# Spreading 1/den of a token chunk over the feature partitions: one DMA with a repeated source, in place of four DMAs with strided targets

## The chip, the cores and the metric

The kernel runs on one core of a Trainium2 chip. The metric is the time on the device in microseconds (us), the median of several executions. Next to each time stands the mean clock granted to TensorE, as a share of full speed. PE is TensorE's matmul side, PEld its weight loads, DVE is VectorE, ACT is ScalarE, SP is SyncE; SPq is the queue in which SP issues DMAs. L586 is line 586 of the kernel. In the profile's lines `ek` is the buffer that holds the result of the spread (`rdb(c)` is a slice of it), `ps<-W,HG` are the products with `W2`, and `ps<-Msb,PQ` the products with `PQ`.

## The reference, cut to what matters

A block of two parallel branches on a normalised input: a linear attention with 32 heads of width 20, and a dense layer of 1536 features with GELU. There are 2048 tokens of width 640, all in bf16.

```python
def _A_ref(x, wqkv, wo):                       # linear attention
    # ... q, k, v = split of x @ wqkv
    phi = lambda t: jnp.where(t > 0, t + 1, jnp.exp(t)) + 1e-6
    pq, pk = phi(q), phi(k)
    kv = jnp.einsum("bhsd,bhse->bhde", pk, v)
    z = jnp.einsum("bhsd->bhd", pk)
    num = jnp.einsum("bhqd,bhde->bhqe", pq, kv)
    den = jnp.einsum("bhqd,bhd->bhq", pq, z)[..., None] + 1e-6
    return (num / den) @ wo                    # heads joined again, cut here
# ...
xn = _layernorm(x)
return x + _A_ref(xn, A_wqkv, A_wo) + _B_ref(xn, B_w1, B_b1, B_w2, B_b2)
```

What matters here is `den`: one number for each token and head. Every feature of `pq` has to be multiplied by the 1/den of its head.

## The kernel before

The kernel holds `pq` transposed: features on the partitions, tokens along the row. The features are ordered so that partition p of each of the five tiles belongs to head p // 4. `den` comes out of a matmul with one head on one partition: rows 32c to 32c+31 of `rden` are the 32 heads of token chunk c (512 tokens). To scale `pq`, row h must reach the four partitions 4h to 4h+3. That is the spread. DMAs do it, on the SyncE queue:

```python
def den_step(b):
    # ... 20 matmuls give den for all four chunks in one bank, cut
    Pl.ins(v, lambda e: e.tensor_single_scalar(den_sb[:], bank(b), 1e-6, ALU.add), ...)   # arguments cut
    Pl.ins(v, lambda e: e.reciprocal(rden[:], den_sb[:]), reads=[r_den], writes=[r_rden])

def rden_scale(c):                       # VectorE: five pieces of 128 x 512
    cc = slice(c * CW, (c + 1) * CW)
    for j in range(DT):
        Pl.ins(v, lambda e, j=j: e.tensor_tensor(out=PQ[:, j, cc], in0=PQ[:, j, cc], in1=rdb(c), op=ALU.mult),
               reads=r_rdb[c] + [r_PQ[c][j]], writes=[r_PQ[c][j]])

def rden_dma(c):                         # SyncE: the spread
    for i in range(4):
        Pl.ins("sync", lambda e, i=i: e.dma_start(rdb(c)[i:P:4, :], rden[H * c:H * (c + 1), :]),
               reads=[r_rden], writes=[r_rdb[c][i]] + ([r_rdb[0][i]] if c == 3 else []), dma=True)
```

The order of work at the end of the kernel decides when the spread is wanted. A tile is 128 tokens; its output is twelve products with `W2` (dense branch), which need no `den`, and five with the scaled `PQ` (attention branch), each done as two matmuls. The `W2` products that PE can do while the spread is on its way are called its cover.

```python
m_step(bs[1:4])
den_step(bs[3])
for t in range(1, 4):
    out_w2(t, b=bs[t])            # W2 products of tiles 1, 2, 3: work that needs no den
ring[0] = bs[0]
rden_dma(0)
rden_scale(0)
rden_dma(1)
for t in range(4):
    out_fin(t, bs[t])             # PQ products of tiles 0 to 3, eviction, store
    if t == 2:
        rden_scale(1)
for t in range(4, NT - 1):
    b = out_w2(t)
    if t in (6, 10):
        rden_scale({6: 2, 10: 3}[t])
    out_fin(t, b)
    if t in (4, 7):
        rden_dma({4: 2, 7: 3}[t])
```

## Time and profile before

| | before |
|---|---|
| time, first 3 runs | 208.4 us (207.85 to 208.42) |
| span in the profile | 206.8 us, clock 1.00 |
| PE busy | 203.2 us, 98% |
| one DMA of the spread | 32 KB, 0.59 us to issue, lands after 1.9 us |

First, who is busy, and what ended last. From the page of the kernel before, parts 1 and 4 (busy time, share of the span and number of instructions; then the chain of work that ended last, by engine):

```profile
PE 203.2 (98%) x1588; PEld 140.3 (68%) x1588; DVE 112.3 (54%) x231; ACT 73.1 (35%) x141; POOL 21.1 (10%) x59
...
PE 96%; DMA 3%; ACTq 0%; DVE 0%; issue 0%
```

The chain is nearly all PE. Its 3% of DMA is the first load of weights; no `rden` DMA and no scaling is on it.

Then the stretch where the first spread happens. The timeline of the kernel before, of VectorE, SyncE and PE in turn (start in us, duration in us, engine, line, operation, number of instructions, and in brackets the idle time before and what ended it):

```profile
134.94 3.35 DVE L568 RECIPROCAL rden<-den_sb 128x512 bf16<-128x512 f32 x1
142.18 1.77 DVE L575 TENSOR_TENSOR PQ<-PQ,ek 128x512 bf16<-128x512 bf16 x5 [3.89 <-DMA ek<-rden]
...
138.32 5.01 SPq L586 DMA_DIRECT2D ek<-rden  x8
...
134.09 9.95 PE L615 MATMUL ps<-W,HG 128*128 128x320 bf16 x72
143.88 5.60 PE L615 MATMUL ps<-Msb,PQ 128*128 128x320 bf16 x40
```

The reciprocal ends at 138.29 us, SyncE issues eight DMAs in 5.01 us (chunks 0 and 1; about 0.63 us each), and VectorE waits 3.89 us for the first four. But PE has 72 matmuls of cover to do from 134.09 us, and goes over to the `PQ` products at 143.88 us with no bracket behind its line: it did not wait. The first scaled piece was ready at about 142.62 us (142.18 + 0.44).

The view of the DMAs of the kernel before has for each kind of issue its number, KB each and the median us from issue to landing:

```profile
DMA packets 24043, 18.32 MB, mean 89 GB/s; under 512 B 10584, under 2 KB 24024, under 8 KB 24024
...
ek<-rden SPq DMA_DIRECT2D x16, 32.0 KB, 1.9
```

The sixteen DMAs of the spread carry 512 KB of the 18.32 MB; each is small, and its 1.9 us can hardly be due to its size, as the 160 KB stores land after 1.8 us.

### The profile page before, as it was taken

What the parts mean: (1) busy time and instruction counts of PE and PEld (TensorE: products, weight loads), DVE (VectorE), ACT (ScalarE), POOL (GpSimd) and SP (SyncE); (2) the same over time, 40 slices, a digit from 0 to 9 for tenths busy, and PEclk for the clock granted to TensorE, in tenths of its full rate; (3) what the DMA queues carried; (4) which work ended last, traced back from release to release, by engine and by line L of the source; (5) the groups of instructions that cost most, each with busy time, mean ns of one, the idle gap of its engine ahead of it and who ended that gap; (6) DMA issues with size and microseconds to landing.
All of it is one profiled execution on the core that took longest, in us unless ns stands there. A gap on an engine that the chain in (4) does not pass through costs nothing.

```text
span 206.8 us, 3962 instructions
## 1 busy us (share of the span) xinstructions
PE 203.2 (98%) x1588; PEld 140.3 (68%) x1588; DVE 112.3 (54%) x231; ACT 73.1 (35%) x141; POOL 21.1 (10%) x59
## 2 busy tenths in 40 slices
PE   7999999999999999999999999999999999999996
PEld 2799987444457777777756556677777777777775
DVE  4589970000007888999288888574863522522332
ACT  2689887666676555111153554400000000000000
POOL 3235568000022000000000000000000000000000
DMA  5999668998000000000300001931111111001002
GB/s 173 338 355 116 105 128 108 376 318 310 3 0 0 0 0 3 0 3 0 63 0 5 0 0 25 373 117 50 64 66 57 56 47 56 32 32 36 32 32 63
DMA packets 24043, 18.32 MB, mean 89 GB/s; under 512 B 10584, under 2 KB 24024, under 8 KB 24024
## 3 DMA queue, kind: packets, MB, share of 16 engines
q1 hardware_dynamic: 23344, 17.57, 29.8%
q10 hardware_dynamic: 680, 0.49, 0.9%
q8 instruction: 12, 0.20, 0.4%
q14 instruction: 7, 0.06, 0.1%
HBM read 12.62 MB, written 2.62 MB: 74 GB/s over the span
## 4 chain that ended last, share of the span: by engine, by line
PE 96%; DMA 3%; ACTq 0%; DVE 0%; issue 0%
PE ps L615 34%; PE ps L352 25%; PE ps L473 11%; PE ps L512 11%; PE ps L524 10%; DMA W<-in_B_w_dram 3%; PE ps L651 2%; PE ps L551 1%; PE ps L533 1%; PE ps L562 1%; PE ps L382 0%; PE ps L336 0%; ACTq L233 0%; DVE out_sb L654 0%
## 5 line engine op out<-in xcount | busy, mean ns | idle before, releaser
L352 PE MATMUL ps<-xnT,W 128*128 128x128 bf16 (+2 forms) x435 | 52.0, 282 | 0.0
L615 PE MATMUL ps<-W,HG 128*128 128x320 bf16 x360 | 51.0, 299 | 0.0
L352 PEld LDWEIGHTS ps<-xnT,W 128*128 128x128 bf16 x435 | 35.5, 98 | 15.7
L615 PEld LDWEIGHTS ps<-W,HG 128*128 128x128 bf16 x360 | 35.1, 98 | 14.2 <-issue 0.4
L356 ACT ACTIVATE HG<-ps,b1c 128x128 bf16<-128x128 f32 (+2 forms) x87 | 40.0, 492 | 12.6 <-PE ps L352 10.4
L634 DVE TENSOR_TENSOR out_sb<-ps,xnT 128x640 bf16<-128x640 f32 x15 | 12.4, 825 | 33.8 <-PE ps L615 33.6
L460 ACT ACTIVATE ek<-ps 128x512 bf16<-128x512 f32 (+1 forms) x36 | 23.2, 644 | 20.3 <-PE ps L524 11.1
L461 DVE TENSOR_SCALAR ek<-ek 128x512 bf16<-128x512 bf16 (+1 forms) x36 | 10.9, 304 | 33.7 <-ACT ek L460 32.6
L615 PE MATMUL ps<-Msb,PQ 128*128 128x320 bf16 x150 | 22.3, 299 | 0.0
L524 PE MATMUL ps<-xnT,Wqkv 128*128 128x512 bf16 x100 | 21.9, 379 | 0.0
L473 PE MATMUL ps<-Wqkv,xnT 128*128 128x320 bf16 x160 | 21.9, 299 | 0.0
L512 PE MATMUL ps<-xPK,xn_tm 128*128 128x320 bf16 x160 | 21.9, 299 | 0.0
L473 PEld LDWEIGHTS ps<-Wqkv,xnT 128*128 128x128 bf16 x160 | 15.7, 98 | 6.2
L512 PEld LDWEIGHTS ps<-xPK,xn_tm 128*128 128x128 bf16 x160 | 15.7, 98 | 6.1
L615 PEld LDWEIGHTS ps<-Msb,PQ 128*128 128x128 bf16 x150 | 14.7, 98 | 5.7
L524 PEld LDWEIGHTS ps<-xnT,Wqkv 128*128 128x128 bf16 x100 | 11.7, 118 | 9.5
L308 DVE BATCH_NORM_STATS2 stats<-xPK 128x6 f32<-128x320 bf16 x32 | 13.6, 466 | 2.8 <-DMA xPK<-in_A_x_dram 2.7
L463 DVE SCALAR_TENSOR_TENSOR PQ<-ps,ek 128x512 bf16<-128x512 f32 x20 | 13.8, 692 | 2.1
L463 DVE SCALAR_TENSOR_TENSOR xPK<-ps,ek 128x640 bf16<-128x640 f32 x16 | 13.2, 825 | 1.7
L499 DVE TENSOR_TENSOR Msb<-Msb,xPK 128x640 f32<-128x640 f32 x14 | 11.6, 825 | 0.5
L318 POOL TENSOR_TENSOR rstd<-aggr,mhalf 128x1 f32<-128x1 f32 x16 | 9.1, 568 | 8.9 <-DVE aggr L316 8.9
L516 ACT ACTIVATE W<-ps 128x640 bf16<-128x640 f32 x5 | 3.5, 703 | 18.2 <-PE ps L512 18.2
(61 smaller groups left out, 93.4 us busy)
## 6 DMA issues: line engine op xcount, KB each, us to landing
xnT<-in_A_x_dram SPq DMA_DIRECT2D x4, 640.0 KB, 6.8
Wqkv<-in_A_wqkv_dram SPq DMA_DIRECT2D x3, 800.0 KB, 6.9
out_dram<-out_sb SPq DMA_DIRECT2D x15, 160.0 KB, 1.8
W<-in_B_w_dram SPq DMA_DIRECT2D x1, 1920.0 KB, 15.4
W<-in_B_w_dram SPq DMA_DIRECT2D x3, 480.0 KB, 7.2
xPK<-in_A_x_dram SPq DMA_DIRECT2D x2, 640.0 KB, 8.6
Wo<-in_A_wo_dram SPq DMA_DIRECT2D x1, 800.0 KB, 10.8
xPK<-in_A_x_dram SPq DMA_DIRECT2D x4, 160.0 KB, 4.3
```

The costliest lines, as they stand in the source:

```text
L308: Pl.ins(v, lambda e: e.bn_stats(stats[:, s, 6 * h:6 * h + 6], x_in[:, t, h * HW:(h + 1) * HW]), reads=[r_x[t]], writes=[r_stats[s][h]])
L352: Pl.ins("tensor", [(lambda e, k=k: e.matmul(bank(b, 0, w), W1[:, k, jb * P:(jb + 1) * P], xnT[:, k, tok], start=(k == 0), stop=(k == DT - ...
L356: Pl.ins("scalar", lambda e: e.activation(HG[:, jb, tok], bank(b, 0, w), ACT.Gelu_apprx_tanh, bias=b1c[:, jb:jb + 1]), reads=[B_[b], r_b1c ...
L460: Pl.ins("scalar", lambda e: e.activation(e2, src, ACT.Exp), reads=br, writes=[r_ek[s]])
L461: Pl.ins(v, lambda e: e.tensor_scalar(et, et, 1.0, 1e-6, ALU.min, ALU.add), reads=[r_ek[s]], writes=[r_ek[s]])
L463: Pl.ins(v, lambda e: e.scalar_tensor_tensor(out=d2, in0=src, scalar=0.0, in1=e2, op0=ALU.max, op1=ALU.add), reads=br + [r_ek[s]], writes= ...
L473: fns.append(lambda e, k=k, h=h, b=b, t=t: e.matmul(bank(b + h, 0, HW), xnT[:, k, t * P:(t + 1) * P], Wqkv[:, k, D + h * HW:D + (h + 1) * ...
L499: Pl.ins(v, lambda e, t=t: e.tensor_tensor(out=zsum, in0=zsum, in1=PK[:, t, :], op=ALU.add), reads=[r_PK[t], r_zsum], writes=[r_zsum])
L512: Pl.ins("tensor", [(lambda e, t=t, h=h, b=b, f=f: e.matmul(bank(b + h, 0, HW), xn_tm[:, t, f * P:(f + 1) * P], PK[:, t, h * HW:(h + 1) * ...
L524: Pl.ins("tensor", [(lambda e, k=k, j=j, b=b: e.matmul(bank(b), Wqkv[:, k, j:D:DT], xnT[:, k, cc], start=(k == 0), stop=(k == DT - 1))) fo ...
L615: return lambda e: e.matmul(bank(b + h, 0, HW), l, r[:, h * HW:(h + 1) * HW], start=(i == 0), stop=(i == JT + DT - 1))
L634: Pl.ins(v, lambda e: e.tensor_tensor(out=halves(out_sb[:, s, :]), in0=pair(b), in1=halves(x_res[:, t, :]), op=ALU.add), reads=B_[b:b + 2] ...
```

## The change

The intent is to send 4 DMAs where there were 16, each with its row read four times. The target is then simply all 128 partitions in order.

```diff
             for j in range(DT):
                 Pl.ins(v, lambda e, j=j: e.tensor_tensor(out=PQ[:, j, cc], in0=PQ[:, j, cc], in1=rdb(c), op=ALU.mult),
-                       reads=r_rdb[c] + [r_PQ[c][j]], writes=[r_PQ[c][j]])
+                       reads=[r_rdb[c], r_PQ[c][j]], writes=[r_PQ[c][j]])
 
         # ... cut
-        r_rdb = [[R_("rdb%d_%d" % (c, i)) for i in range(4)] for c in range(NC)]
+        r_rdb = [R_("rdb%d" % c) for c in range(NC)]
         # ... cut
         def rden_dma(c):
-            for i in range(4):
-                Pl.ins("sync", lambda e, i=i: e.dma_start(rdb(c)[i:P:4, :], rden[H * c:H * (c + 1), :]),
-                       reads=[r_rden], writes=[r_rdb[c][i]] + ([r_rdb[0][i]] if c == 3 else []), dma=True)
+            src = rden[H * c:H * (c + 1), :].unsqueeze(1).to_broadcast([H, 4, CW])
+            Pl.ins("sync", lambda e: e.dma_start(rdb(c), src),
+                   reads=[r_rden], writes=[r_rdb[c]] + ([r_rdb[0]] if c == 3 else []), dma=True)
```

## The prediction

> **What bounds the kernel now.** TensorE. The table of engines shows PE busy 203.2 us of the 206.8 us span (98%). The chain of waits is 96% PE, 3% the first weight load and one 0.29 us VectorE instruction at the end: no DMA of `rden` and no scaling of `PQ` is on it. The view by stretches shows PE busy in all of 134.1 to 200.2 us, at clock 1.00.
>
> **What the change touches.** Sixteen DMAs `ek<-rden` of 32 KB (four for each token chunk) become four of 128 KB. The DMA table and the line's view show that one of the sixteen takes 0.59 us on the SyncE queue (median) and lands 1.9 us after issue (1.8 to 3.4). The bytes are the same.
>
> - *Removed:* 12 issues, 12 x 0.59 = 7 us of SyncE queue time, with 12 semaphores and waits. SyncE's queue is on no chain here: worth 0.
> - *Moved:* for chunk 0 the reciprocal ends at 138.3 us, the fourth issue starts near 140.2 us, and VectorE starts the first scaling of `PQ` at 142.18 us after waiting 3.9 us (waits, timeline). With one issue the chunk should land 1.9 to 2.5 us after 138.3; the wait should shrink to some 2.0 to 2.7 us, and the scaling start 1.3 to 2 us earlier. Chunk 1 lands earlier too; chunks 2 and 3 are sent several us before VectorE wants them.
> - *Added:* only a larger transfer in one issue. A 160 KB store over 128 partitions has an issue time of 0.33 us and lands after 1.8 us, so 128 KB in one piece should cost at most some tenths more than 32 KB. The Trainium skill, "DMA: Bandwidth & Descriptors", section "Rules for kernel authors", warns that a leading broadcast dimension of c < 16 copies confines a DMA to c engines. Here the repeat of four stands behind 32 partitions, and the target leads with 128, so by that page the spread over 16 engines stays; no run here shows it yet.
>
> **How much is on the critical path.** None. PE wants the scaled `PQ` first at about 143.7 us, when the `W2` products of tiles 0 to 3 are done. The first scaled piece is there at 142.6 us and another follows every 0.35 us; PE takes one each 0.27 us. The spare time is about 1.1 us for the first piece and 0.8 us for the fifth, and the groups show PE idle 0.0 there. The change makes that some 2.5 us, and more spare time on an engine nobody waits for is worth nothing. The work of VectorE, ScalarE and PE is the same.
>
> **Prediction.** 208.2 us (before: 208.4; 207.85 to 208.42 in three runs), range 207.5 to 208.9. Chances: faster by over 2%: 0.01; within 2%: 0.97; slower by over 2%: 0.02.
>
> **What would show each step.**
> - `ek<-rden`: 4 issues of 128 KB, landing after 2 to 2.5 us.
> - VectorE's wait for them falls from 3.9 to 2.0 to 2.7 us; the first scaling starts near 140.5 us.
> - PE busy near 203.2 us, no wait for `PQ`, its first `PQ` product still near 143.7 us; the chain still 96% PE.
>
> **What would make it wrong.** If the repeated source makes the single DMA slow (few engines, tiny descriptors), the spare time goes: PE stalls once chunk 0 lands later than about 4.9 us after the first issue, against 3.8 now. The later chunks have more time, so the loss would be one excess: a 10 us landing would cost some 5 us, 2.4%. The changed instruction stream or fewer semaphores could shift the time by tenths of a us.

## The result, and the profile after

| | before | after |
|---|---|---|
| time, median of 6 runs | 208.29 us (207.85 to 208.42) | 208.11 us (207.91 to 208.29) |
| ratio | | 0.9993, 95% interval 0.998 to 1.0006 |
| clock | 1.00 | 1.00 |
| span in the profile | 206.8 us | 206.8 us |
| `rden` DMAs | 16 of 32 KB | 4 of 128 KB |
| VectorE's wait for the first | 3.89 us | 2.73 us |

A ratio is the mean time of one kernel's runs over that of the other's of the same rounds, so it is not quite the ratio of the medians quoted. Executions over 1.5% slower than the fastest of the same kernel are left out of the means. The interval includes 1: within 0.2% the time is the same.

The page of the kernel after, parts 1 and 4:

```profile
PE 203.7 (98%) x1588; PEld 140.6 (68%) x1588; DVE 112.2 (54%) x231; ACT 73.2 (35%) x141; POOL 21.2 (10%) x59
...
PE 96%; DMA 3%; ACTq 0%; DVE 0%; issue 0%
```

The timeline of the kernel after, of VectorE, SyncE and PE, in the same stretch:

```profile
135.01 3.35 DVE L568 RECIPROCAL rden<-den_sb 128x512 bf16<-128x512 f32 x1
141.09 1.77 DVE L575 TENSOR_TENSOR PQ<-PQ,ek 128x512 bf16<-128x512 bf16 x5 [2.73 <-DMA ek<-rden]
...
138.39 1.58 SPq L586 DMA_DIRECT2D ek<-rden  x2
...
134.16 9.95 PE L615 MATMUL ps<-W,HG 128*128 128x320 bf16 x72
143.95 5.60 PE L615 MATMUL ps<-Msb,PQ 128*128 128x320 bf16 x40
```

The view of the DMAs of the kernel after, for the whole span:

```profile
DMA packets 23851, 18.32 MB, mean 89 GB/s; under 512 B 10392, under 2 KB 23832, under 8 KB 23832
...
ek<-rden SPq DMA_DIRECT2D x4, 128.0 KB, 2.6
```

The same view from 138 to 143.5 us only, where two DMAs of the spread run on queue q1 and nothing else does (packets, MB, share of 16 engines):

```profile
q1 hardware_dynamic: 288, 0.26, 21.3%
```

The change did what it was meant to do: VectorE's wait became 1.16 us shorter, and SyncE spends 1.58 us on the first two chunks in place of 5.01. PE goes over to `PQ` 9.79 us after the start of its 72 matmuls in both kernels (143.88 - 134.09 and 143.95 - 134.16), without a wait in either.

The packets also speak for all 16 DMA engines taking part. Two DMAs of 128 rows of 1 KB are 256 packets, and 288 - 256 = 32 is 16 more for each DMA. Over the span, 24043 - 23851 = 192 = 12 x 16 small packets went away with twelve DMAs. That fits the Trainium skill, "DMA: Bandwidth & Descriptors", section "Why a DMA increments its semaphore by 16 and not by 1": every engine that takes part writes the semaphore once. That the 16 extra packets are these writes is this reading of the counts; no view names them.

### The profile page after: what moved, and what is told of

Its sections match the earlier page's. It is cut to its first block, busy times and chain, and to the rows that moved or that the text cites. A ratio compares the mean times of both kernels' runs of the same rounds, so it can differ in the third digit from the quotient of the medians.

```text
span 206.8 us, 3936 instructions
## 1 busy us (share of the span) xinstructions
PE 203.7 (98%) x1588; PEld 140.6 (68%) x1588; DVE 112.2 (54%) x231; ACT 73.2 (35%) x141; POOL 21.2 (10%) x59
## 2 busy tenths in 40 slices
DMA packets 23851, 18.32 MB, mean 89 GB/s; under 512 B 10392, under 2 KB 23832, under 8 KB 23832
## 4 chain that ended last, share of the span: by engine, by line
PE 96%; DMA 3%; ACTq 0%; DVE 0%; issue 0%
PE ps L615 34%; PE ps L352 25%; PE ps L512 11%; PE ps L473 11%; PE ps L524 10%; DMA W<-in_B_w_dram 3%; PE ps L651 2%; PE ps L551 1%; PE ps L533 1%; PE ps L562 1%; PE ps L382 1%; PE ps L336 0%; ACTq L233 0%; DVE out_sb L654 0%
## 5 line engine op out<-in xcount | busy, mean ns | idle before, releaser
L615 PE MATMUL ps<-W,HG 128*128 128x320 bf16 x360 | 51.0, 299 | 0.0
L615 PEld LDWEIGHTS ps<-W,HG 128*128 128x128 bf16 x360 | 35.1, 98 | 14.2 <-issue 0.4
L615 PE MATMUL ps<-Msb,PQ 128*128 128x320 bf16 x150 | 22.3, 299 | 0.0
L615 PEld LDWEIGHTS ps<-Msb,PQ 128*128 128x128 bf16 x150 | 14.7, 98 | 5.7
```

Source lines behind the costliest of these rows:

```text
L615: return lambda e: e.matmul(bank(b + h, 0, HW), l, r[:, h * HW:(h + 1) * HW], start=(i == 0), stop=(i == JT + DT - 1))
```

## The experiments

**Theory, spare time.** PE goes over to `PQ` at the later of two moments: when its cover work is done, and when the first scaled piece is there. In the kernel before, the first piece was there more than a microsecond before the cover was done, so bringing the piece forward is worth nothing, and putting it off costs nothing until the spare time is used up.

**Rival 1, on the path.** The spread does count, and something else ate the gain, such as the longer landing of the big DMA.

**Rival 2, no dependence.** The time does not depend on the spread at all in this range.

All runs below were correct, and all times are of the fast state, or single runs whose state is unknown. In copies with added lines the line of the `PQ` and `W2` products moves from L615 to L619, that of the spread from L586 to L589.

### Later: chunk 0 in eight DMAs, and in sixteen

```diff
-            for i in range(4):
-                Pl.ins("sync", lambda e, i=i: e.dma_start(rdb(c)[i:P:4, :], rden[H * c:H * (c + 1), :]),
+            m = H // PIECES[c]                     # PIECES = [2, 1, 1, 1] for eight, [4, 1, 1, 1] for sixteen
+            for n in range(4 * PIECES[c]):
+                i, q = n % 4, n // 4
+                Pl.ins("sync", lambda e, i=i, q=q: e.dma_start(rdb(c)[4 * m * q + i:4 * m * (q + 1):4, :],
+                                                               rden[H * c + m * q:H * c + m * (q + 1), :]),
                        # ... reads and writes, cut
```

What was expected of eight:

> Chunk 0 in eight DMAs of 16 KB in place of four of 32 KB, the other chunks as before. Issues follow each other every 0.63 us in the kernel before, so the eighth should be issued near 142.7 us, land near 144.6 us, and the last scaled piece of chunk 0 be done near 146.4 us. THEORY SPARE TIME (the spread may come up to about 1.1 us later than before at no cost, only the excess counts): PE ends the PQ products of tile 0 near 146.7 us where it would have ended them near 145.1 us, so it stalls about 1.6 us, time 209.9 us, ratio 1.008. RIVAL ON THE PATH (every us of the spread counts, and the change's 1.1 us were eaten by something else, such as the longer landing): the 2.4 us later spread cost 2.4 us, ratio 1.012. RIVAL NO DEPENDENCE (nobody waits for the spread within this range): ratio 1.000.

Measured with eight: 209.47 us (209.26 to 209.73), the kernel before beside it 208.25; ratio 1.005, interval 1.0018 to 1.0082. (One of the eleven runs of before took 210.23 us; it pulls that mean up. The medians differ by 1.22 us.) The timeline of PE in the kernel with eight:

```profile
133.86 9.95 PE L619 MATMUL ps<-W,HG 128*128 128x320 bf16 x72
144.95 5.86 PE L619 MATMUL ps<-Msb,PQ 128*128 128x320 bf16 x40 [1.13 <-DVE PQ L575]
```

Now PE has a bracket: 1.13 us idle, waiting for the scaling. The group behind it takes 5.86 us in place of 5.60, at clock 1.00, because the pieces come one by one and PE waits a little for each. Together that is 1.39 us. Putting the scaling off by 2.5 us, counted from the start of the 72 matmuls, cost about half of that. The theory's ratio of 1.008 lies in the measured interval; the rivals' 1.012 and 1.000 lie outside it. Both rivals fail.

What was expected of sixteen:

> Chunk 0 in sixteen DMAs of 8 KB, the other chunks as before. The sixteenth should be issued near 147.7 us, land near 149.6 us, the last scaled piece be done near 151.4 us. SPARE TIME: PE stalls about 6.6 us (151.7 against 145.1 us), time 214.9 us, ratio 1.032, and the step from the eight-DMA kernel is 5.0 us, all of the further delay. ON THE PATH: 7.4 us, ratio 1.036. NO DEPENDENCE: ratio 1.000.

Measured with sixteen: 217.09 us (216.75 to 217.82), ratio 1.0418, interval 1.0386 to 1.045; mean clock 0.984. It cost 8.84 us where 6.6 were expected. By the time alone, this run can't tell the theory from the rival "on the path" (7.4 us). The timeline of PE in this kernel:

```profile
134.26 9.95 PE L619 MATMUL ps<-W,HG 128*128 128x320 bf16 x72
151.15 7.40 PE L619 MATMUL ps<-Msb,PQ 128*128 128x320 bf16 x40 [6.93 <-DVE PQ L575]
```

Its view by stretches (stretch, its length, busy time of PE, PEld, DVE, ACT and POOL, granted clock, DMA share, GB/s):

```profile
147.00:149.00 2.00, 0.00 (x0) 0.00 (x0) 0.00 (x0) 0.00 (x0) 0.00 (x0) 0.75 0.06 12
149.00:151.00 2.00, 0.00 (x0) 0.00 (x0) 0.34 (x1) 0.00 (x0) 0.00 (x0) 0.50 0.10 25
151.00:153.00 2.00, 1.85 (x8) 1.00 (x9) 1.83 (x6) 0.00 (x0) 0.00 (x0) 0.50 0.19 51
```

The idle time of 6.93 us is near the expected one. The rest is 7.40 - 5.60 = 1.80 us in the matmuls right after it: the granted clock falls to 0.50 while PE is idle and stays there when it starts again. 6.93 + 1.80 = 8.73 us, close to the 8.84 measured. Not all of the 1.80 us need be the clock's: in the kernel with eight, the same group was 0.26 us longer at clock 1.00.

### Later where there is much spare time: chunks 2 and 3 in sixteen DMAs each

The same edit with PIECES = [1, 1, 4, 4].

> Chunks 2 and 3 in sixteen DMAs of 8 KB each, chunks 0 and 1 in four as before. The sixteen issues take about 10 us of the SyncE queue; chunk 2 should land near 166.7 us, where VectorE wants it at 159.5 us, and chunk 3 near 180.6 us, wanted at 178.0 us. VectorE waits some 7 and 3 us, and the output stores behind them are issued up to 6 us late. SPARE TIME (PE wants chunk 2 only near 175.7 us and chunk 3 near 194.1 us): the time is that of the kernel before, ratio 1.000 within 0.002. RIVAL ON THE PATH (each wait of VectorE for the spread counts, wherever it is): some 10 us, ratio 1.05.

Measured: 208.12 us (207.79 to 208.22) against 208.18; ratio 0.9992, interval 0.9978 to 1.0005. The timeline of VectorE in this kernel:

```profile
167.69 1.77 DVE L575 TENSOR_TENSOR PQ<-PQ,ek 128x512 bf16<-128x512 bf16 x5 [8.37 <-DMA ek<-rden]
...
184.57 1.82 DVE L575 TENSOR_TENSOR PQ<-PQ,ek 128x512 bf16<-128x512 bf16 x5 [6.77 <-DMA ek<-rden]
```

PE's first `PQ` groups of chunk 2 (tile 8) and of chunk 3 (tile 12) in this kernel have no bracket, so PE did not wait:

```profile
170.80 1.52 PE L619 MATMUL ps<-Msb,PQ 128*128 128x320 bf16 x10
...
189.27 1.52 PE L619 MATMUL ps<-Msb,PQ 128*128 128x320 bf16 x10
```

The expectation had these moments one tile too late (175.7 and 194.1 us; in the kernel before they are 171.05 and 189.52). Still the first scaled pieces, 0.44 us after the scaling starts, were there 2.67 and 4.26 us before PE took them.

VectorE waits 8.37 and 6.77 us where it did not wait in the kernel before (its only wait for the spread there is the 3.89 us of chunk 0), and the time does not move. A wait is not a cost because it is long; it costs when the engine on the chain runs out of other work.

### Exposed: one tile of cover in place of three, with four DMAs and with one

Here PE is made to wait for the spread, in both forms. If the 1.1 us are real, they must now appear in the time.

```diff
-        for t in range(1, 4):
-            out_w2(t, b=bs[t])
+        out_w2(1, b=bs[1])
         ring[0] = bs[0]
         rden_dma(0)
         rden_scale(0)
         rden_dma(1)
         for t in range(4):
+            if t >= 2:
+                out_w2(t, b=bs[t])
             out_fin(t, bs[t])
```

With four DMAs:

> The kernel before, with only one tile of W2 products (tile 1) instead of three between the den step and the first PQ product; tiles 2 and 3 come after the first two tiles are finished. The work is the same. PE should be ready for PQ near 137.4 us and have to wait: it would end tile 0 near 138.7 us unhindered, and can end it only near 144.3 us, after the fifth scaled piece. SPARE TIME: about 5.5 us longer than the kernel before, ratio 1.027, and VectorE's wait for the four DMAs still 3.9 us. A rival that says PE is not held by the spread at all: ratio 1.00.

With one:

> The same reordering, with the changed spread (one DMA for a chunk). SPARE TIME: now PE does wait for the spread, so the 1.1 us by which one DMA brings the scaling forward (142.18 to 141.09 us in the two traces) must come out in the time: about 4.4 us over the kernel before, ratio 1.021, and 1.1 us (0.5%) below the same order with four DMAs. RIVAL EATEN ELSEWHERE (the earlier scaling is an appearance, for instance the pieces are not all there, or the larger DMA slows something else by as much): no difference between the two.

Measured: four DMAs 216.00 us (215.44 to 216.37), ratio 1.0359, interval 1.0327 to 1.039. One DMA 214.27 us (213.44 to 215.50), ratio 1.0285, interval 1.0247 to 1.0322. The timeline of PE with four DMAs, then with one:

```profile
134.19 3.43 PE L615 MATMUL ps<-W,HG 128*128 128x320 bf16 x24
142.77 5.51 PE L615 MATMUL ps<-Msb,PQ 128*128 128x320 bf16 x20 [5.14 <-DVE PQ L575]
```

```profile
134.01 3.43 PE L615 MATMUL ps<-W,HG 128*128 128x320 bf16 x24
141.42 5.25 PE L615 MATMUL ps<-Msb,PQ 128*128 128x320 bf16 x20 [3.97 <-DVE PQ L575]
```

PE's idle time differs by 5.14 - 3.97 = 1.17 us, as it should, so the gain is real where it is exposed. But both kernels cost over 1.5 us more than expected, and the medians differ by 1.73 us. The clock had fallen again: the twenty `PQ` matmuls took 5.51 and 5.25 us, where twenty took 2.88 us before. From the views by stretches, four DMAs first, then one:

```profile
141.00:143.00 2.00, 0.23 (x1) 0.13 (x2) 0.72 (x3) 0.00 (x0) 0.00 (x0) 0.59 0.21 57
```

```profile
139.00:141.00 2.00, 0.00 (x0) 0.00 (x0) 0.07 (x1) 0.00 (x0) 0.00 (x0) 0.61 0.57 113
```

The runs list the mean clock of each. All six with four DMAs had 0.984. With one DMA, three had 0.984 (214.45 to 215.50 us) and three 0.992 (213.44 to 214.09 us). At the same 0.984 the medians are 216.00 and 215.02 us, 0.98 us apart, near the 1.1 expected; the rest of the 1.73 us goes with the three runs whose mean clock was higher.

### The clock as a separate suspect: dummy matmuls in the gap

Matmuls on a buffer of zeros, into a bank not in use, fill most of the gap.

```diff
         out_w2(1, b=bs[1])
+        Pl.ins("tensor", [lambda e: e.matmul(bank(bs[2]), warm[:, 0:P], warm[:], start=True, stop=True)
+                          for _ in range(16)], reads=[r_warm], writes=[B_[bs[2]]])
```

> The order with one tile of W2 products as cover, four DMAs, and sixteen dummy matmuls of 128x512 on PE (0.22 us apart, so about 3.5 us) in the stretch where PE would wait. In the same order without them PE was idle 5.1 us, its clock fell to 0.50 for some 6 us, and the run was 7.75 us longer than the kernel before where 5.5 were expected. THEORY CLOCK (the excess of over 2 us is the lower clock after a long idle time of PE): the dummy matmuls leave 1.6 us of idle time, the clock stays 1.00, and the time is about 5.4 us over the kernel before, 213.6 us, ratio 1.026. RIVAL (the excess is the order itself: later stores, VectorE or PSUM waits): time as without them, 216.0 us, ratio 1.036.

> The same with one DMA per chunk. CLOCK: clock 1.00, about 4.3 us over the kernel before, 212.5 us, ratio 1.021, and 1.1 us (0.5%) below the filled kernel with four DMAs: where PE waits for the spread at an undisturbed clock, the change is worth just the 1.1 us by which the scaling starts earlier. RIVAL: 214.3 us as without the dummy matmuls, and 1.7 us below the one with four.

Measured: four DMAs 215.68 us (213.81 to 216.15), ratio 1.0352, interval 1.0321 to 1.0383, so a miss as it stands. One DMA 212.96 us (212.57 to 214.32), ratio 1.0245, interval 1.0222 to 1.0269; near what was expected. With four, PE was idle 1.79 us and then took the pieces as they came, and the clock still fell to 0.50 in the profiled run (timeline of PE, then a stretch):

```profile
142.80 4.76 PE L615 MATMUL ps<-Msb,PQ 128*128 128x320 bf16 x20 [1.79 <-DVE PQ L575]
...
145.00:147.00 2.00, 2.00 (x9) 1.13 (x8) 1.16 (x2) 0.00 (x0) 0.00 (x0) 0.50 0.17 60
```

Five of its six runs had a mean clock of 0.992 to 0.998. The one run at 1.00 took 213.81 us, near the expected 213.6. So the four-DMA kernel got 21 dummy matmuls, and the one-DMA kernel was run again beside it.

> The filled order with four DMAs again, with 21 dummy matmuls in place of 16, so that PE is idle only about 0.6 us before the first scaled piece, as long as in the filled kernel with one DMA and 16. With 16, five of six runs of the four-DMA kernel had a clock below 1.00 (0.992 to 0.998 as the mean of the span) and took 215.5 to 216.2 us; the one run at 1.00 took 213.81 us. CLOCK: now all runs at 1.00, about 213.7 us. RIVAL (the order itself): some runs still at 215.5 to 216.2 us.

> The filled kernel with one DMA and 16 dummy matmuls again, unchanged, to stand beside the other on the same chip in the same rounds. CLOCK: 212.6 us at clock 1.00, 1.1 us below the kernel with four DMAs: an exposed spread, at an undisturbed clock, is worth its 1.1 us and no more. RIVAL (one DMA gains more than its earlier landing, as the 1.7 us of the unfilled pair suggested): 1.7 us or more.

Measured: four DMAs 213.99 us (213.93 to 214.09, four runs, all at clock 1.00), ratio 1.0279, interval 1.0266 to 1.0293. One DMA 214.19 us (212.39 to 214.65), ratio 1.0269, interval 1.0239 to 1.0298: by its median a miss of 1.6 us. The first is settled: without the fall of the clock the four-DMA order costs 5.81 us (213.99 against 208.18), near the 5.5 that the theory says. PE's 462 matmuls from the first `PQ` product on took 63.18 us in its chain, shown below, and 65.57 us in the chain of the same order without dummy matmuls: the lower clock cost 2.39 us there. For the second, see the chain that ended last in both kernels, in order of time (start in us, duration, what), from the scaling to the last instruction. With four DMAs:

```profile
142.33 0.44 DVE PQ L575
142.77 0.04 issue
142.81 63.18 PE ps L615 x462
206.00 4.67 PE ps L651 x51
210.67 0.02 issue
210.69 0.29 DVE out_sb L654
```

With one:

```profile
141.29 0.44 DVE PQ L575
141.73 0.05 issue
141.77 63.18 PE ps L615 x462
204.96 4.67 PE ps L651 x51
209.63 0.02 issue
209.66 0.29 DVE out_sb L654
```

PE takes the same 63.18 and 4.67 us in both, and was idle 0.62 and 0.51 us before them. Up to the last instruction of any engine, one DMA is 1.03 us ahead (209.66 against 210.69), although PE's `W2` matmuls had started 0.14 us later (134.37 against 134.23). What followed was not the same: the last store, 32 KB, landed 3.1 us after issue in the one-DMA profile and 1.5 us after in the other. The runs of the one-DMA kernel fall in two groups of spans, 211.1 and 211.6 us, and 212.8 to 213.4 us. Why the last store was late, and whether it was in each of the slower runs, stays open: only one of them has a trace. The clock is not the whole of it: two of the four slower runs had a mean clock of 0.999 and 0.997, the other two 1.00. The identical kernel run earlier had five of six spans at 211.3 to 211.9 us; its median was 4.88 us over the kernel before, against the 5.81 us of four DMAs with 21, so 0.93 us less, though in other rounds. The claim that an exposed spread gains its 1.1 us therefore rests on the traces, on the lower group, on this comparison and on the 0.98 us of the unfilled pair at equal clock; the medians of this last pair don't show it.

### One rule for all the timelines

Count from the start of PE's `W2` matmuls in each trace (134.09 us before, 134.16 us after, and so on).

| kernel | cover ends | scaling starts | PE starts on `PQ` |
|---|---|---|---|
| before | 9.79 | 8.09 | 9.79 |
| after | 9.79 | 6.93 | 9.79 |
| chunk 0 in eight | 9.79 | 10.60 | 11.09 |
| chunk 0 in sixteen | 9.79 | 16.40 | 16.89 |
| one tile of cover, four DMAs | short | 8.09 | 8.58 |
| one tile of cover, one DMA | short | 6.92 | 7.41 |
| the same, filled, four (21) | short | 8.10 | 8.58 |
| the same, filled, one (16, repeat) | short | 6.92 | 7.40 |

The cover's end is read from before and after, as PE's start on `PQ` there, and carried over to the two kernels with the same cover; so the rows that test the rule are the others. PE starts at the later of 9.79 us and 0.49 us after the scaling starts, to 0.01 us in all rows. The two filled kernels left out fit as well (four with 16: 8.20 and 8.68; one with 16, first run: 6.93 and 7.42). So the spare time was 9.79 - 0.49 - 8.09 = 1.21 us before and is 2.37 us after.

### Why one DMA of 128 KB lands later than one of 32 KB

In the traces the big DMA took 2.6 us (2.6 to 2.9), the small ones 1.9 (median; 1.8 to 3.4). To find out why, single DMAs of 128 KB were added to the changed kernel between the stores, each into a dead buffer, so the output stays right.

```diff
             if t in (4, 7):
                 rden_dma({4: 2, 7: 3}[t])
+            if t in PROBES:
+                probe(t)       # one DMA of 128 KB (or 32 KB) into a dead buffer; each form twice
```

> The changed kernel, with eight single DMAs added on the SyncE queue between the output stores, each alone between two of them, into a dead buffer: a plain copy of 128 rows of 1 KB (128 source partitions); the change's own form, 32 source partitions each read four times; 32 source partitions with four different rows of 1 KB each; and the old form, 32 rows to every fourth partition. It asks why one DMA of 128 KB landed 2.6 to 2.9 us after issue, against 1.9 us of one of 32 KB. SIZE: all three 128 KB forms land after about 2.6 us, the small one after 1.9 us. REPEATED SOURCE: only the form that reads the same row four times takes 2.6 us, the other two about 1.9 us. FEW SOURCE PARTITIONS: the repeated form and the four different rows take 2.6 us, the plain copy about 1.9 us. The time of the kernel stays within 0.3% of the kernel before in all three.

> Again the changed kernel with single DMAs of 128 KB added between the stores, to a dead buffer, to tell apart why a source of 32 neighbouring partitions landed after 2.6 us and one of 128 after 2.0 us. Sources: every fourth partition with four rows of 1 KB each; partitions 0 to 31 with four rows; 0 to 63 with two rows; 0 to 15 with each row read eight times. THEORY PORTS (what counts is which ports of the memory the source partitions reach): every fourth partition lands like the full copy, 2.0 us; 0 to 63 like 0 to 31, 2.6 us; 0 to 15 clearly later, some 3.2 to 3.8 us. RIVAL COUNT (fewer source partitions are slower whichever they are): every fourth 2.6 us, 0 to 63 about 2.3 us. RIVAL FORM (the third dimension of the access pattern costs 0.6 us): 2.6 us in all four.

The theory of ports in the second text comes from the page of the Trainium skill that is cited below.

Measured, with issue to landing as minimum, median and maximum of two. Lines of the views by source line of the first probe kernel, in the order: plain copy from 128 partitions; 32 partitions, each row four times; 32 partitions, four different rows each; the old form of 32 KB.

```profile
DMA to landing us min/median/max: 2.0/2.0/2.0
...
DMA to landing us min/median/max: 2.6/2.6/2.6
...
DMA to landing us min/median/max: 2.6/2.7/2.8
...
DMA to landing us min/median/max: 1.8/2.2/2.6
```

Of the second, in the order: every fourth partition, four rows each; partitions 0 to 31, four rows; 0 to 63, two rows; 0 to 15, each row eight times.

```profile
DMA to landing us min/median/max: 2.0/2.0/2.0
...
DMA to landing us min/median/max: 2.5/2.6/2.6
...
DMA to landing us min/median/max: 2.3/2.3/2.4
...
DMA to landing us min/median/max: 3.1/3.1/3.1
```

It isn't the size alone: the same 128 KB from 128 partitions land after 2.0 us. It isn't the repetition: four different rows are as slow. It isn't the count of source partitions or the form of the pattern: 32 partitions spread over the whole range land after 2.0 us. What counts is that the 32 are neighbours. The Trainium skill, "SBUF — State Buffer", section "Door 1: The DMA port swizzle", says that partitions 0 to 31 reach 8 of the 16 ports, 0 to 127 all of them; 0 to 15 reach four by its table. The order of 2.0, 2.6 and 3.1 us agrees with that. Its further statement, that 0 to 63 do no better than 0 to 31, is not what these runs show: 2.3 us, in between. Why is open. The two small DMAs of 32 KB, at 1.8 and 2.6 us, are too few and too far apart to say anything. With 32 neighbours as the source the size does count: 2.6 us for 128 KB, against a median of 1.9 us for 32 KB in the kernel before.

The kernels themselves took 207.79 and 208.95 us, single runs beside 208.18 and 208.08. In the second, PE's first weights had come 0.9 us later than in the changed kernel (the first step of its chain took 6.43 us there, 5.52 in the changed kernel), which accounts for it.

## Why the prediction was right or wrong

- *PE bounds the kernel and the spread is off its path.* Right, and shown: the same moment of going over to `PQ` in both traces, and a kernel whose spreads of chunks 2 and 3 come many us late costs nothing.
- *Spare time of 1.1 us before, 2.5 us after.* Right in mechanism and nearly in size: 1.21 and 2.37 us, from the rule above. The kernel with eight, which uses it up, pays only for the excess; the one with sixteen pays for the excess and for a lower clock (last point).
- *208.2 us, within 2%.* Right: 208.11 us, inside the range of 207.5 to 208.9.
- *Landing after 2 to 2.5 us, scaling 1.3 to 2 us earlier.* Somewhat off: 2.6 to 2.9 us, and 1.16 us earlier, counted from the same start. The term that was too small is "128 KB in one piece should cost at most some tenths more than 32 KB", which measured 0.7 us. It was taken from a store whose source spans all 128 partitions, while the source here is 32 neighbours. The wait of VectorE came out at the edge of what was said (2.73 against 2.0 to 2.7). Being off the path, the error did not reach the time.
- *The spread over 16 engines stays.* Right, by the count of packets: 16 beside the 128 rows of each DMA.
- *If the landing were too slow, the loss would be "one excess".* Only half right. Short excesses cost what they last. Long ones cost more: the kernel with sixteen DMAs lost 8.84 us for an idle time of 6.93, because the clock fell to 0.50 and PE's next matmuls were slow. The Trainium skill, "TensorE: Matmul & The Clock Gate", section "Part 1: The HAM clock gate", describes this fall after an idle window of about 3.4 us. Two traces agree: worked out from the stretches shown, in which the clock goes from 1.00 to 0.50, it fell about 3.8 us after PE's last cover matmul with sixteen DMAs (148.0 against 144.21 us) and about 3.7 us after it with one tile of cover and four (141.36 against 137.62). Two don't: with one tile of cover and one DMA it fell after about 2.0 us (139.44 against 137.44), and a gap of 1.79 us, followed by work paced by VectorE, was enough as well.

## What to carry to other kernels

Before shortening a wait, compare when its result is ready with when the engine on the chain first wants it; time won on the near side of that moment only adds to the spare time. Test such spare time by putting the result off, which costs nothing until the margin is used up, and by taking the cover away, which shows what the shortening would be worth. When an experiment makes TensorE idle, look at its clock before reading the difference as a wait.

## What the Trainium skill lacked or had wrong

- "SBUF — State Buffer", "Door 1: The DMA port swizzle": it gives partitions 0 to 63 the bandwidth of 0 to 31, 4% apart as measured at 1 MiB. For a copy of 128 KB within SBUF the runs show 2.0 us to landing from 0 to 127, 2.3 from 0 to 63, 2.6 from 0 to 31 and 3.1 from 0 to 15. The page gives no times of such short copies by range of partitions.
- "DMA: Bandwidth & Descriptors", "Rules for kernel authors": its row on using all 16 engines takes a repeat as the leading dimension as its example. For a repeat behind 32 partitions its rule, by the slowest dimension, gives 16 engines, which fits the packets here (288 for two DMAs of 128 rows). What the page lacks is the time of such a copy: it landed no later than four different rows from the same 32 partitions (2.6 against 2.6 to 2.7 us).
- "TensorE: Matmul & The Clock Gate", "Part 1: The HAM clock gate": it gives an idle window of about 3.4 us. Here the clock fell 2.0 us after PE's last matmul in one trace, and a gap of 1.79 us with paced matmuls behind it brought the clock to 0.50 in the profiled run, and below 1.00 as a mean in five of six runs, while gaps of 1.13 and 0.62 us left the profiled runs at 1.00. The page calls the window free-running, and its section on a second failure mode names frequent short idle times, without a figure; how little work in a window is enough it doesn't say.
